# A transformer kernel on one core: sink-free attention scores get their mask from TensorE, banks are handed out in written order, and TensorE issues in written order

## The chip, the cores and the metric

One Trainium2 chip, one of its NeuronCores. The metric is the device time of one execution in microseconds (us). TensorE is called PE in the profile, with its weight loads listed apart as PEld; VectorE is DVE, ScalarE is ACT, GpSimd is POOL, SyncE (which issues most DMAs here) is SP.

## The reference

The kernel computes three things in a row. Attention works on 2 batches, 8 heads, 768 positions and 64 channels per head, with a window of 128 positions and 4 sink positions that every row may see:

```python
keep = is_sink | in_window          # in_window: 0 <= row - column < 128
scores = np.where(keep, scale * (q @ k.T), -1e9)
a = np.exp(scores - max(scores)); a = a / (sum(a) + 1e-9)
x = (a @ v) laid out as 1536 tokens x 512 channels
x = (silu(x @ w_gate) * (x @ w_val)) @ w_out            # d_ff 1536
g = x @ w_in; x = max(g, 0) + alpha * min(g, 0)         # d_ff 2048
out = x @ w_out2
```

## The kernel before

The attention is cut into 24 groups (class `Group`): one pair of heads by two blocks of 128 rows. A group that begins at row 0 of its batch (`i0 == 0`) needs no separate sink columns, because its keys already hold them; there are 8 of these sink-free groups. The 16 others carry a sink strip (`self.sink`). `ORDER` puts the groups in three passes of 8; a pass makes 512 tokens. The first pass holds just the 8 sink-free groups, first the four head pairs of batch 0, then the four of batch 1 (L814).

`attention` (L322) is a software pipeline over x = 0 to 26, written in this order for each x:

- `scores(x)`: PE multiplies q and k in fp32 into one PSUM bank for each head and block. DVE adds the mask and finds the row minimum of the negated scores in one instruction (L223), ACT takes the exponential of that bank and sums it (L227).
- `values(x-3)`: PE multiplies the transposed probabilities with v (L313, L316), ACT and DVE split the result into a high and a low half, `xh` (L805) and `xl` (L806).
- `flips(x-2)`: PE transposes probabilities (L272), and a sink strip (L295), into PSUM; ACT or DVE copies them out (L278, L280, L283), POOL cuts triangles (L284, L288).
- `norm(x)`: DVE adds and inverts the sums (L243, L244), POOL scales the probabilities (L250, L259).

Between these, `fast` weaves in the first feed-forward layer (`Moe1.unit`). From x = 10 on, after the first pass is done, `product()` issues one step of it: 12 matmuls of 128x512 in the fp32r format, of which one `pg` (gate), one `pv` (value) or one `po` (output) bank is made. There is one such step for each x before `values`, and one more after the flips of each x in `TWICE`. A gate bank needs all four head pairs of its pass: its 12 matmuls are three for each pair (`proj`, L609). A step also calls `st.tick()`, which converts one weight tile: ACT L520, DVE L536, L539 and L542, ACT L550, POOL or DVE L557. In the first pass only four weights are converted (`EARLY`).

DVE issues in written order (`manual_schedule`, L799). On PE, ACT and POOL a planner chooses the order ahead of time, and it chooses which of the 8 PSUM buffers a tile gets (one pool `ps`, L865). The chip then runs each engine's list in that order, with semaphores. After the attention the rest of the feed-forward work follows (`mix`), in which PE has nothing to wait for.

Of the kernel before, what the change touches and what calls it, by code (L numbers as in the profile page):

```python
# [16 lines left out]
P = 128  # L17
# [3 lines left out]
KD = DM // P  # L21
# [21 lines left out]
TWICE = (10, 12, 14, 16, 18, 20, 22, 25)  # L43
# [14 lines left out]

def setup(nc, tc, ctx, g):
# [7 lines left out]
    g.mask_0 = const.tile([P, P], F32, name="mask_0")  # L67
    g.mask_1 = const.tile([P, 2 * P], F32, name="mask_1")
    g.above = const.tile([P, P], I32, name="above")
    g.zero = const.tile([P, T], mybir.dt.bfloat16, name="zero")  # L70


def warm(nc, g, n):

    nc.vector.memset(g.zero, 0.0)
    ps = g.ps_m.tile([P, 512], F32, tag="ps", name="warm")
# [43 lines left out]
def first_masks(nc, g):  # L120
    win, snk = g.win, g.snk
    prev, cur = win[:, 0:P], win[:, P:]
    nc.vector.scalar_tensor_tensor(out=win, in0=g.rel, scalar=g.wd, in1=g.ge, op0=ALU.is_lt, op1=ALU.mult)
    nc.vector.tensor_scalar(out=snk, in0=g.key, scalar1=g.ns, scalar2=None, op0=ALU.is_lt)
    nc.vector.tensor_tensor(out=g.mask_0, in0=cur, in1=snk, op=ALU.max)
    bias(nc.vector, g.mask_0, g.mask_0)
    nc.vector.tensor_tensor(out=g.mask_1[:, 0:P], in0=prev, in1=snk, op=ALU.max)
    nc.vector.tensor_copy(g.mask_1[:, P:], cur)
    bias(nc.vector, g.mask_1, g.mask_1)
# [26 lines left out]
class Group:  # L156
    def __init__(self, nc, g, qk, vp, vs, b, hp, i0, put, cs, blk):
        self.nc, self.g = nc, g
        self.b, self.hp, self.i0, self.put = b, hp, i0, put
        self.cs, self.blk = cs, blk  # L160
        self.h0 = 2 * hp
        self.j0 = max(0, i0 - 1)
        self.nk = i0 + NG - self.j0
        self.sink = i0 + NG > 2
        self.off = 1 if i0 == 0 else 0
        self.qk_src, self.v_src = (x[min(i0, 1)] for x in (qk, vp))
        n = b * NPAIR + hp if i0 == 0 else (b * 2 + i0 // NG - 1) * NPAIR + hp
        self.qk_src, self.v_src = self.qk_src[n], self.v_src[n]
        self.vs_src = vs[b * NPAIR + hp]
        if self.sink:  # L170
# [29 lines left out]
    def scores(self, t):  # L200
        nc, g = self.nc, self.g
        i = self.i0 + t
        w, blk, sp, kk = self.blocks(t)
        lo, first = self.kpos[kk], P if sp is not None else 0
        if t == 0:
            self.ssum = g.st_p.tile([P, NG, 2], F32, tag="ssum", name="ssum")
            self.prb = g.pr_p.tile([P, 3 * 2 * P], F32, tag="pr", name="pr")
        p0 = self.prb_at(t)
        mask = g.mask_0 if i == 0 else g.mask_1 if i == 1 else g.mask_b if kk % 2 else g.mask_a
        pss = []  # L210
        for e in range(2):
            ps = g.ps_s.tile([P, 512], F32, tag="ps", name="ps_s")
            pss.append(ps)
        qs, ks = slice(self.qpos[t], self.qpos[t] + P), slice(lo, lo + first + w)
        for e in range(2):
            r = slice(e * D, (e + 1) * D)
            nc.tensor.matmul(pss[e][:, :first + w], self.th[r, qs], self.th[r, ks], start=True, stop=True)
        for e in range(2):
            ps = pss[e][:, first:first + w]
            if first:  # L220
                nc.vector.copy_predicated(ps[:, blk[0]:blk[0] + P], g.above, pss[e][:, 0:P])
            col = (self.b * H + self.h0 + e) * NQ + i
            nc.vector.tensor_tensor_reduce(  # L223
                out=ps, in0=ps, in1=mask, scale=-SCALE, scalar=3.0e38,
                op0=ALU.add, op1=ALU.min, accum_out=g.nb[:, col:col + 1],
            )
            nc.scalar.activation(  # L227
                self.prb[:, p0 + e * w:p0 + (e + 1) * w], ps, AF.Exp,
                bias=g.nb[:, col:col + 1], scale=-1.0, accum_out=self.ssum[:, t, e:e + 1]
            )  # L230
# [31 lines left out]
    def flip(self, t):  # L262
# [5 lines left out]
        ps = g.ps_t.tile([P, 512], F32, tag="ps", name="ps_p")  # L268
        for e in range(2):
            for x, c in enumerate(blk):  # L270
                y = (e * nb + x) * P
                nc.tensor.transpose(ps[:, y:y + P], self.pr(t, e, c, P), g.ident)  # L272
        b0 = max(0, 2 * t - self.off)
# [18 lines left out]
        if t == NG - 1 and self.sink:  # L292
            self.pts = g.pt_p.tile([P, P], F32, tag="pts", name="pts")
            ps = g.ps_t.tile([P, 512], F32, tag="ps", name="ps_p2")
            nc.tensor.transpose(ps[:, 0:P], self.sk.rearrange("p x s -> p (x s)"), g.ident)  # L295
            nc.scalar.activation(self.pts, ps[:, 0:P], AF.Copy)

    def values(self):
        nc, g, i0, n = self.nc, self.g, self.i0, NG
        xp = g.ps_x.tile([P, 512], F32, tag="ps", name="xp")  # L300
# [18 lines left out]
        self.put(xp[:, :n * P], self.hp, self.cs)  # L319


def attention(groups, begin):  # L322
# [12 lines left out]
    for x in range(n + LAG + 1):  # L335
        if x < n:
            for t in range(NG):
                groups[x].scores(t)
# [16 lines left out]
def verdict(nc, g):  # L355
# [9 lines left out]
    ps = g.ps_t.tile([P, 512], F32, tag="ps", name="ps_flag")  # L365
# [8 lines left out]
def dense(nc, tc, g, q, k, v, b):  # L374
    with ExitStack() as ctx:
# [17 lines left out]
        for hp in range(NPAIR):  # L393
# [4 lines left out]
            for e in range(2):  # L398
# [14 lines left out]
                for t in range(NQ):  # L413
                    ps = g.ps_t.tile([P, 512], F32R, tag="ps", name="dps_k")
# [6 lines left out]
            for i in range(NQ):  # L421
                ts = slice(i * P, (i + 1) * P)
                xp = g.ps_x.tile([P, 512], F32, tag="ps", name="dxp")
                for e in range(2):
                    src = sp.tile([P, S], F32, tag="src", name="dsrc")
                    for c0, n in ((0, 512), (512, 256)):
                        ps = g.ps_s.tile([P, 512], F32, tag="ps", name="dps_s")
# [17 lines left out]
                    for t in range(0, NQ, 2):  # L445
                        ps = g.ps_t.tile([P, 512], F32, tag="ps", name="dps_p")
# [161 lines left out]

def proj(nc, ps, w, xh, xl):  # L609
    wh, wl = w  # L610
    for kk in range(KD):
        c = slice(kk * P, (kk + 1) * P)
        nc.tensor.matmul(ps, wh[:, c], xh[:, kk], start=(kk == 0), stop=False)  # L613
        nc.tensor.matmul(ps, wh[:, c], xl[:, kk], start=False, stop=False)  # L614
        nc.tensor.matmul(ps, wl[:, c], xh[:, kk], start=False, stop=(kk == KD - 1))  # L615
# [14 lines left out]
class Moe1:  # L630
    def __init__(self, nc, g, st, base, xs, put):
        self.nc, self.g, self.st, self.base, self.xs, self.put = nc, g, st, base, xs, put
        self.accs = {}

    def unit(self, c, b):
# [10 lines left out]
        for x in range(0, CHUNK, 2):  # L646
            pair = hidden_pair(g)
            pss, sgs = [], []
            for r in range(2):
                ps = g.ps_m.tile([P, 512], F32, tag="ps", name="pg")  # L650
# [4 lines left out]
            for ps in pss:  # L655
                sg = g.t_p.tile([P, T], F32, tag="sg", name="sg")
                nc.scalar.activation(sg, ps, AF.Silu)
                sgs.append(sg)
            yield
            for r in range(2):  # L660
                hh, hl = (t[:, r] for t in pair)
                ps = g.ps_m.tile([P, 512], F32, tag="ps", name="pv")
                proj(nc, ps, st.get(at(1, x + r)), xh, xl)
                hid = g.t_p.tile([P, T], F32, tag="hid", name="hid")
                nc.vector.tensor_tensor(out=hid, in0=ps, in1=sgs[r], op=ALU.mult)  # L665
                split_hidden(nc, hid, hh, hl)
# [9 lines left out]
        for m in range(KD):  # L676
            mc = slice(m * P, (m + 1) * P)
            ps = g.ps_m.tile([P, 512], F32, tag="ps", name="po")
# [8 lines left out]
            else:  # L687
                nc.vector.tensor_tensor(out=av, in0=ps, in1=av, op=ALU.add)
            if c == nch - 1:
                split_hidden(nc, av, yh[:, m], yl[:, m])  # L690
# [8 lines left out]
class Moe2:  # L699
# [4 lines left out]
    def unit(self, c, b):  # L704
# [6 lines left out]
        for x in range(CHUNK):  # L711
# [4 lines left out]
            ph = g.ps_m.tile([P, 512], F32, tag="ps", name="ph")  # L716
# [15 lines left out]
        for t in range(T // P):  # L732
            ps = g.ps_m.tile([P, 512], F32, tag="ps", name="pf")
# [40 lines left out]

def fast(nc, tc, ctx, g, lim, alpha, qk, vp, vs, w_gate, w_val, w_out, x2_in, x2_out, out):
# [21 lines left out]
    with ExitStack() as inner:  # L797
        attention_pools(nc, tc, inner, g)
        inner.enter_context(tc.manual_schedule(engines={mybir.EngineType.DVE}))  # L799
# [14 lines left out]
        groups[:2 * NPAIR] = groups[0:2 * NPAIR:2] + groups[1:2 * NPAIR:2]  # L814
# [9 lines left out]
        for at, x, last in attention(groups, (begin_a, begin_b, begin_c)):  # L824
            done = max(0, last + (at != "before values"))
            if at == "values" and done in (per, 2 * per):
                ready.append(m1.unit(0, done // per - 1))
            if done < per:
                if at == "flips" and st.n_conv < EARLY:
                    st.tick(1 + (done > 1))  # L830
            elif at == "before values" or at == "flips" and x in TWICE:
                product()
    st.idle_pool = False
    for u in ready:
        for _ in u:
            st.tick()
# [6 lines left out]
def general(nc, tc, g, q, k, v, w_gate, w_val, w_out, x2_in, x2_out, out):  # L843
    g.exact = True
    with ExitStack() as ctx:
        xp = ctx.enter_context(tc.tile_pool(name="gx", bufs=1))
# [15 lines left out]
def build(nc, tc, q, k, v, w_gate, w_val, w_out, x2_in, x2_out, alpha, lim, qk0, qk1, v0, v1, vs, out):  # L862
    with ExitStack() as ctx:
        g = Ctx()
        ps = ctx.enter_context(tc.tile_pool(name="ps", bufs=8, space=PSUM))  # L865
        g.ps_m = g.ps_s = g.ps_t = g.ps_x = ps
# [71 lines left out]
```

## Time and profile before

| | us |
|---|---|
| median of 3 runs | 680.9 (680.4 to 681.8) |
| the profiled execution | 680.56 |
| its span, first to last instruction | 678.8 |
| PE busy in the span | 657.4 (97%) |
| DVE busy | 391.7 (58%) |
| ACT busy | 297.8 (44%) |
| POOL busy | 79.9 (12%) |

The span leaves out 1.76 us of the profiled execution's time. Busy times are of records; consecutive matmuls overlap in them, so how fast PE runs is read from the distance between the starts of matmuls. The mean granted PE clock over the span is 0.987 of full speed.

### The profile page before, as it was taken

Reading aid. Unit: us, or ns where it says so; the run is one execution under the profiler, and the core shown is the slowest. Engines: PE = TensorE matmul, PEld = TensorE weight load, DVE = VectorE, ACT = ScalarE, POOL = GpSimd, SP = SyncE. Lnnn points to the kernel's source line nnn. Section 1 sums busy time; section 2 is a strip of 40 time slices with the busy share of each in tenths; the row PEclk is TensorE's granted clock in tenths of the full one; section 3 lists DMA queues with packets and bytes.
Section 4 is the critical chain, followed back from the end, with each engine's and each line's share of the span. In section 5 each row is a group of like instructions: output and inputs, shape, how many; then the busy total and the mean of one; then the engine's idle time right before and its main releaser. Section 6 shows DMA issues by size and latency. Waiting matters only on the chain.

```text
span 678.8 us, 8589 instructions
## 1 busy us (share of the span) xinstructions
PE 657.4 (97%) x3098; PEld 519.5 (77%) x3098; DVE 391.7 (58%) x880; ACT 297.8 (44%) x680; POOL 79.9 (12%) x137
## 2 busy tenths in 40 slices
PE   7889889999999999999999999999999999999996
PEld 4555666767788888888888888888888888888885
DVE  5896858444289932389432789419834744334332
ACT  4778765656366612155221546336622333112320
POOL 3554644333100000000000000000000000000000
PEclk8989899999999999999999999999999999999998
DMA  9653535200045520045200034203400000000111
GB/s 264 180 169 115 166 114 168 69 24 24 1 155 186 169 79 1 0 125 181 68 0 1 33 124 129 89 1 93 156 1 0 1 0 1 1 0 8 55 63 67
DMA packets 37203, 52.29 MB, mean 77 GB/s; under 512 B 4384, under 2 KB 28960, under 8 KB 37152
## 3 DMA queue, kind: packets, MB, share of 16 engines
q1 hardware_dynamic: 34944, 51.65, 24.0%
q8 instruction: 26, 0.43, 0.2%
q10 hardware_dynamic: 2208, 0.01, 0.2%
q14 instruction: 25, 0.20, 0.1%
HBM read 48.51 MB, written 3.15 MB: 76 GB/s over the span
## 4 chain that ended last, share of the span: by engine, by line
PE 84%; DVE 7%; ACT 5%; issue 1%; POOL 1%; DMA 1%; SPq 0%; ACTq 0%; POOLq 0%
PE ph L615 6%; PE ph L613 6%; PE pf L739 6%; PE pf L737 6%; PE pf L738 6%; PE ph L614 6%; PE po L681 5%; PE po L682 5%; PE po L683 5%; PE pv L613 4%; PE pg L613 4%; PE pv L615 4%; PE pv L614 4%; PE pg L614 4%; PE pg L615 4%; PE xp L313 2%
## 5 line engine op out<-in xcount | busy, mean ns | idle before, releaser
L626 ACT ACTIVATE hh<-hid 128x512 fp32r<-128x512 f32 x84 | 53.1, 632 | 70.5 <-DVE hid L665 41.2
L627 DVE TENSOR_TENSOR hl<-hid,hh 128x512 fp32r<-128x512 f32 x84 | 57.9, 689 | 36.5 <-ACT hh L626 36.4
L613 PE MATMUL ph<-yh,wh 128*128 128x512 f32 x192 | 74.8, 390 | 0.0
L615 PE MATMUL ph<-yh,wl 128*128 128x512 f32 x192 | 74.7, 389 | 0.0
L737 PE MATMUL pf<-wh,hh 128*128 128x512 f32 x192 | 74.7, 389 | 0.0
L738 PE MATMUL pf<-wl,hh 128*128 128x512 f32 x192 | 74.7, 389 | 0.0
L614 PE MATMUL ph<-yl,wh 128*128 128x512 f32 x192 | 74.7, 389 | 0.0
L719 ACT ACTIVATE neg<-ph,sal 128x512 f32<-128x512 f32 x48 | 33.0, 687 | 93.4 <-PE ph L615 93.4
L739 PE MATMUL pf<-wh,hl 128*128 128x512 f32 x192 | 72.1, 389 | 0.0
L550 ACT ACTIVATE wh<-w_m 128x512 fp32r<-128x512 f32 x68 | 42.6, 630 | 55.8 <-DVE w_m L542 17.4
L721 DVE SCALAR_TENSOR_TENSOR hid<-ph,sig,neg 128x512 f32<-128x512 f32 x48 | 35.9, 749 | 38.4 <-ACT neg L719 38.0
L613 PE MATMUL pg<-xh,wh 128*128 128x512 f32 x144 | 57.6, 401 | 0.0
L613 PE MATMUL pv<-xh,wh 128*128 128x512 f32 x144 | 56.9, 395 | 0.3 <-ACT pt L283 0.3
L614 PE MATMUL pg<-xl,wh 128*128 128x512 f32 x144 | 57.0, 396 | 0.0
L615 PE MATMUL pg<-xh,wl 128*128 128x512 f32 x144 | 56.6, 393 | 0.0
L681 PE MATMUL po<-hh,wh 128*128 128x512 f32 x144 | 56.5, 394 | 0.0
L614 PE MATMUL pv<-xl,wh 128*128 128x512 f32 x144 | 56.2, 391 | 0.0
L682 PE MATMUL po<-hh,wl 128*128 128x512 f32 x144 | 56.2, 391 | 0.0
L615 PE MATMUL pv<-xh,wl 128*128 128x512 f32 x144 | 56.1, 390 | 0.0
L744 DVE TENSOR_TENSOR acc<-pf,acc 128x512 f32<-128x512 f32 x36 | 23.2, 686 | 52.0 <-PE pf L739 52.0
L683 PE MATMUL po<-hl,wh 128*128 128x512 f32 x144 | 53.2, 390 | 0.0
L557 DVE TENSOR_TENSOR wl<-w_m,wh 128x512 fp32r<-128x512 f32 x56 | 38.2, 686 | 21.6 <-ACT wh L550 21.5
(106 smaller groups left out, 1198.0 us busy)
## 6 DMA issues: line engine op xcount, KB each, us to landing
w_raw<-in_moe_w_out SPq DMA_DIRECT2D x28, 512.0 KB, 3.4
w_raw<-in_moe_w_in SPq DMA_DIRECT2D x16, 512.0 KB, 3.8
w_raw<-in_moe_w_gate SPq DMA_DIRECT2D x12, 512.0 KB, 3.7
w_raw<-in_moe_w_val SPq DMA_DIRECT2D x12, 512.0 KB, 3.6
th<-in_qk SPq DMA_DIRECT2D x16, 336.0 KB, 3.0
vr<-in_v SPq DMA_DIRECT2D x16, 192.0 KB, 2.4
out<-acc SPq DMA_DIRECT2D x12, 256.0 KB, 2.2
th<-in_qk SPq DMA_DIRECT2D x8, 256.0 KB, 5.5
```

The costliest lines, as they stand in the source:

```text
L550: nc.scalar.activation(wh, m, AF.Copy)
L613: nc.tensor.matmul(ps, wh[:, c], xh[:, kk], start=(kk == 0), stop=False)
L614: nc.tensor.matmul(ps, wh[:, c], xl[:, kk], start=False, stop=False)
L615: nc.tensor.matmul(ps, wl[:, c], xh[:, kk], start=False, stop=(kk == KD - 1))
L626: nc.scalar.activation(hh, hid, AF.Copy)
L627: nc.vector.tensor_tensor(out=hl, in0=hid, in1=hh, op=ALU.subtract)
L681: nc.tensor.matmul(ps, wh[:, mc], hh, start=(x == 0), stop=False)
L682: nc.tensor.matmul(ps, wl[:, mc], hh, start=False, stop=False)
L683: nc.tensor.matmul(ps, wh[:, mc], hl, start=False, stop=(x == CHUNK - 1))
L737: nc.tensor.matmul(ps, hh[:, ts], wh, start=(x == 0), stop=False)
L738: nc.tensor.matmul(ps, hh[:, ts], wl, start=False, stop=False)
L739: nc.tensor.matmul(ps, hl[:, ts], wh, start=False, stop=(x == CHUNK - 1))
```

## The change

PSUM becomes one tile of 8 banks that the kernel hands out itself in the order in which the program is written (`Banks`: the bank given back longest ago is taken first). In the first pass scores have banks 0 to 3, taken by twos, transposes and values have banks 4 to 6, and bank 7 is for the first gate. PE joins DVE in `manual_schedule`, so PE issues in written order too. When the attention is over, the tile is released and an ordinary pool of 8 buffers takes its place; a pool that lands on the bytes of a released one lets all its buffers wait for every user of the old one.

A sink-free group puts both blocks of a head side by side in one bank (128 and 256 columns). PE first writes the mask into it, as the product of an identity and `mask_f`, and adds the scores to it. DVE then takes two row maxima over both heads at once and scales them once; ACT's exponential reads the bank with the scale.

The first pass goes by head pair: batch 0 and batch 1 of pair 0, then of pair 1, and so on. When both groups of a pair are split, `m1.part` issues the three matmuls of that pair for the first gate bank, so that the gate's 12 matmuls stand at x = 4, 6, 8 and 10, and the step at x = 10 has none left. `TWICE` has one entry less. The steps left over after x = 26 are issued inside the region where PE is in written order. The transposed sink strip goes into the bank of the group's second transposes in place of a bank of its own.

```diff
-TWICE = (10, 12, 14, 16, 18, 20, 22, 25)
+TWICE = (10, 13, 16, 18, 20, 22, 25)
...
+class Banks:
+    def __init__(self, pool):
+        self.all = pool.tile([P, 8, 512], F32, name="banks")
+        self.free = list(range(8))
+        self.held = {}
+
+    def take(self, n=1, among=range(8)):
+        for i in self.free:
+            if i % n == 0 and i in among and all(j in self.free for j in range(i, i + n)):
+                break
...
+        for j in range(i, i + n):
+            self.free.remove(j)
...
+    def give(self, ap):
+        self.free += self.held.pop(id(ap))[1]
...
 def identities(nc, g):
     make_identity(nc, g.ident)
+    nc.gpsimd.tensor_copy(g.identr, g.ident)
...
+    bias(nc.vector, g.mask_f[:, 0:P], both)
...
+    bias(nc.vector, g.mask_f[:, P:2 * P], g.rel[:, P:])
+    bias(nc.vector, g.mask_f[:, 2 * P:], cur)
...
+    def free_scores(self):
         nc, g = self.nc, self.g
+        ps = g.banks.take(2, range(4))
+        for e in range(2):
+            nc.tensor.matmul(ps[:, e, :3 * P], g.identr, g.mask_f, start=True, stop=False, skip_group_check=True)
+        cols = [slice(0, P), slice(P, 3 * P)]
+        for t, c in enumerate(cols):
+            for e in range(2):
+                r = slice(e * D, (e + 1) * D)
+                nc.tensor.matmul(
+                    ps[:, e, c], self.th[r, self.qpos[t]:self.qpos[t] + P], self.th[r, 0:(t + 1) * P],
+                    start=False, stop=(t == 1), skip_group_check=True,
+                )
+        top = ps[:, :, 510:512]
+        for t, c in enumerate(cols):
+            nc.vector.tensor_reduce(out=top[:, :, t], in_=ps[:, :, c], axis=AX.X, op=ALU.max)
+        nc.vector.tensor_scalar(out=self.nb, in0=top, scalar1=-SCALE, scalar2=None, op0=ALU.mult)
+        for t, c in enumerate(cols):
+            for e in range(2):
+                self.exp(ps[:, e, c], t, e, SCALE)
+        give(g, ps)
...
-            ps = g.ps_t.tile([P, 512], F32, tag="ps", name="ps_p2")
-            nc.tensor.transpose(ps[:, 0:P], self.sk.rearrange("p x s -> p (x s)"), g.ident)
-            nc.scalar.activation(self.pts, ps[:, 0:P], AF.Copy)
+            nc.scalar.activation(self.pts, ps[:, 2 * P:3 * P], AF.Copy)
...
+    def part(self, kk):
+        if kk == 0:
+            self.begun = bank(self.g, "pg", (7,))
+        proj_part(self.nc, self.begun, self.st.get(self.base), *self.xs[0], kk)
...
-        inner.enter_context(tc.manual_schedule(engines={mybir.EngineType.DVE}))
+        g.banks = Banks(inner.enter_context(tc.tile_pool(name="bank", bufs=1, space=PSUM)))
+        inner.enter_context(tc.manual_schedule(engines={mybir.EngineType.DVE, mybir.EngineType.PE}))
...
-        groups[:2 * NPAIR] = groups[0:2 * NPAIR:2] + groups[1:2 * NPAIR:2]
...
+            if at == "flips" and 0 < done <= per and done % 2 == 0:
+                m1.part(done // 2 - 1)
...
+        while ready:
+            product()
     st.idle_pool = False
-    for u in ready:
-        for _ in u:
-            st.tick()
+    psum_pool(tc, ctx, g)
```

## Rows read from the trace of the kernel before

**Rows 1.** Windows by stage: length; busy us (instructions) PE PEld DVE ACT POOL; PEclk, DMA, GB/s

```profile
0.00:48.50 48.50, 39.66 (x213) 23.92 (x214) 38.36 (x158) 30.55 (x116) 23.50 (x37) 0.89 0.69 204
48.50:182.60 134.10, 127.58 (x725) 90.14 (x724) 74.46 (x260) 82.98 (x235) 56.41 (x100) 0.99 0.29 90
```

**Rows 2.** The same view: a PE gap, the stretch after it, and a dense one

```profile
77.00:79.00 2.00, 0.33 (x1) 0.14 (x1) 1.93 (x5) 1.97 (x5) 0.70 (x1) 1.00 0.51 154
79.00:84.50 5.50, 5.44 (x16) 3.88 (x17) 4.02 (x17) 5.21 (x19) 4.09 (x7) 0.70 0.43 143
...
300.00:400.00 100.00, 100.00 (x443) 82.81 (x442) 58.87 (x101) 35.60 (x62) 0.00 (x0) 1.00 0.21 70
```

**Rows 3.** Waits of PE, 48.5 to 182.6 us: waiting <- waited for: us, times, longest

```profile
PE ps_s L217 <- ACT pr L227: 2.5, 2, 1.5
PE ps_p L295 <- ACT pr L227: 1.7, 1, 1.7
```

**Rows 4.** Timeline of all engines at the start: start, us, instruction, idle before

```profile
5.20 1.34 PE L217 MATMUL ps_s<-th 64*128 64x128 f32 x8
...
6.95 0.52 DVE L105 TENSOR_SCALAR mask<-mask 128x256 f32<-128x256 f32 x1
...
7.38 0.28 DVE L223 CUSTOM_DVE_ANT_0 ps_s<-ps_s,mask 128x128 f32<-128x128 f32 x1
...
7.76 0.37 ACT L227 ACTIVATE pr<-ps_s,nb 128x128 f32<-128x128 f32 x1 [4.75 <-DVE nb L223]
...
10.40 0.17 DVE L243 TENSOR_SCALAR rinv<-ssum 128x4 f32<-128x4 f32 x1 [1.67 <-ACT pr L227]
...
12.82 0.17 DVE L243 TENSOR_SCALAR rinv<-ssum 128x4 f32<-128x4 f32 x1 [0.78 <-ACT pr L227]
```

**Rows 5.** Timeline of DVE, x = 4 (to 25.13) and x = 8

```profile
22.41 0.42 DVE L806 TENSOR_TENSOR xl<-xp,xh 128x256 fp32r<-128x256 f32 x1 [0.84 <-ACT xh L805]
22.75 0.68 DVE L278 COPY pt<-ps_p 128x512 f32<-128x512 f32 x1
23.35 0.42 DVE L536 TENSOR_SCALAR w_m<-w_m 128x512 int32<-128x512 int32 x1
...
25.13 0.17 DVE L243 TENSOR_SCALAR rinv<-ssum 128x4 f32<-128x4 f32 x1
...
41.77 0.42 DVE L806 TENSOR_TENSOR xl<-xp,xh 128x256 fp32r<-128x256 f32 x1
...
43.00 0.28 DVE L221 COPY_PREDICATED ps_s<-above,ps_s 128x128 f32<-128x128 int32 x1
```

**Rows 6.** Waits of DVE up to 48.5 us

```profile
DVE xl L806 <- ACT xh L805: 2.1, 2, 1.3
```

**Rows 7.** Timeline of PE: scores of x = 9, then three stretches of the mixed stage

```profile
38.43 1.16 PE L217 MATMUL ps_s<-th 64*128 64x288 f32 x4
...
120.35 0.87 PE L313 MATMUL xp<-pt,vr 128*64 128x256 f32 x8
...
122.92 0.48 PE L614 MATMUL pg<-xl,wh 128*128 128x512 f32 x1
...
129.72 1.09 PE L313 MATMUL xp<-pt,vr 128*64 128x256 f32 x12
...
131.92 1.24 PE L217 MATMUL ps_s<-th 64*128 64x288 f32 x8
...
136.04 0.87 PE L313 MATMUL xp<-pt,vr 128*64 128x256 f32 x8
```

**Rows 8.** Timeline of all engines: a last output bank of the attention's region

```profile
180.86 0.39 PE L683 MATMUL po<-hl,wh 128*128 128x512 f32 x1
...
181.28 0.60 ACT L686 ACTIVATE acc<-po 128x512 f32<-128x512 f32 x1 [2.12 <-PE po L683]
```

**Rows 9.** Groups by line up to 200 us: changes to Silu's table

```profile
L657 ACT ACT_TABLE_LOAD x8 | 10.3, 1283 | 0.1
```

**Rows 10.** Timeline of POOL: the last cut before the values at 136.04

```profile
134.66 0.41 POOL L288 TENSOR_SCALAR_AFFINE_SELECT pt<-pt 128x256 f32<-128x256 f32 x1
```

More of the change, by code (lines that the diff above doesn't have):

```diff
@@ L56, with bank, give @@
     pass
+class Banks:
[7 more added lines that the diff above has]
+                break
+        else:
+            assert False, self.free
+        for j in range(i, i + n):
+            self.free.remove(j)
+        ap = self.all[:, i:i + n] if n > 1 else self.all[:, i]
+        self.held[id(ap)] = (ap, range(i, i + n))
+        return ap
+    def give(self, ap):
+        self.free += self.held.pop(id(ap))[1]
+def bank(g, name, among=range(8)):
+    return g.banks.take(1, among) if g.banks else g.ps.tile([P, 512], F32, tag="ps", name=name)
+def give(g, ap):
+    if g.banks:
+        g.banks.give(ap)
 def setup(nc, tc, ctx, g):
@@ L169, in __init__ @@
         self.vs_src = vs[b * NPAIR + hp]
+        self.banks = range(8) if self.sink else range(4, 7)
         if self.sink:
@@ L198, in blocks, with begin @@
         return KW, [0], P, kk
-    def scores(self, t):
-        nc, g = self.nc, self.g
-        i = self.i0 + t
-        w, blk, sp, kk = self.blocks(t)
[L204 to L214, printed above, removed]
+    def begin(self):
+        g = self.g
+        self.ssum = g.st_p.tile([P, NG, 2], F32, tag="ssum", name="ssum")
+        self.prb = g.pr_p.tile([P, 3 * 2 * P], F32, tag="pr", name="pr")
+        self.nb = g.nb.rearrange("p (h i) -> p h i", i=NQ)[:, self.b * H + self.h0:][:, :2, self.i0:self.i0 + NG]
@@ new lines, in exp, with scores @@
+    def exp(self, src, t, e, scale):
+        o = self.prb_at(t) + e * src.shape[1]
+        self.nc.scalar.activation(
+            self.prb[:, o:o + src.shape[1]], src, AF.Exp, bias=self.nb[:, e, t:t + 1], scale=scale,
+            accum_out=self.ssum[:, t, e:e + 1],
+        )
+    def scores(self):
+        self.begin()
+        if self.sink:
+            for t in range(NG):
+                self.sink_scores(t)
+        else:
+            self.free_scores()
+    def free_scores(self):
+        nc, g = self.nc, self.g
+        ps = g.banks.take(2, range(4))
[8 more added lines that the diff above has]
+                    start=False, stop=(t == 1), skip_group_check=True,
+                )
+        top = ps[:, :, 510:512]
[5 more added lines that the diff above has]
+                self.exp(ps[:, e, c], t, e, SCALE)
+        give(g, ps)
@@ L215, in scores, with sink_scores @@
+    def sink_scores(self, t):
+        nc, g = self.nc, self.g
+        w, blk, sp, kk = self.blocks(t)
+        lo = self.kpos[kk]
+        pss = [bank(g, "ps_s") for e in range(2)]
+        qs, ks = slice(self.qpos[t], self.qpos[t] + P), slice(lo, lo + P + w)
         for e in range(2):
             r = slice(e * D, (e + 1) * D)
-            nc.tensor.matmul(pss[e][:, :first + w], self.th[r, qs], self.th[r, ks], start=True, stop=True)
+            nc.tensor.matmul(pss[e][:, :P + w], self.th[r, qs], self.th[r, ks], start=True, stop=True)
@@ L227, in scores @@
[L227 to L230, printed above, removed]
+                out=ps, in0=ps, in1=g.mask_b if kk % 2 else g.mask_a, scale=-SCALE, scalar=3.0e38,
+                op0=ALU.add, op1=ALU.min, accum_out=self.nb[:, e, t:t + 1],
+            )
+            self.exp(ps, t, e, -1.0)
+            give(g, pss[e])
     def prb_at(self, t):
@@ L267, in flip @@
         nb = len(blk)
-        ps = g.ps_t.tile([P, 512], F32, tag="ps", name="ps_p")
+        ps = bank(g, "ps_p", self.banks)
         for e in range(2):
@@ L336, in attention @@
         if x < n:
-            for t in range(NG):
-                groups[x].scores(t)
+            groups[x].scores()
         yield "before values", x, x - LAG - 1
@@ L649, in unit @@
             for r in range(2):
-                ps = g.ps_m.tile([P, 512], F32, tag="ps", name="pg")
+                if self.begun is not None and (c, b, x, r) == (0, 0, 0, 0):
+                    pss.append(self.begun)
+                    continue
+                ps = bank(g, "pg")
                 proj(nc, ps, st.get(at(0, x + r)), xh, xl)
```

72 lines of the change are left out of this document (40 added, 32 removed).

## The prediction

> **What bounds the kernel now.** I read the windows by stage first. After the attention PE runs dense, 443 matmuls in 100 us, so 0.226 us for each [rows 2], and nothing in the change touches that stage. What can move lies in two stages. In the *first pass* (to 48.5 us) PE has no feed-forward work; it has records for 39.7 of 48.5 us, and DVE, in written order, is the busiest in effect with 38.4 us, while each of its steps also waits for ACT [rows 1]. This stage is a chain, not a load. In the *mixed stage* (48.5 to 182.6 us) PE is the bound: it idles 134.1 - 127.6 = 6.5 us [rows 1], mostly for a PSUM buffer that an exponential or a Silu still reads (2.5 us of scores, 1.7 us of a transposed sink strip, and smaller ones [rows 3]), and one of these gaps is followed by 5.5 us at a mean clock of 0.70 [rows 2]. With levels of 1.2 and 2.4 GHz that is 3.3 us at the lower one, a loss of 1.65 us. So 8.2 us of the mixed stage are not work. The sum below is made against the profiled execution, 680.56 us (span 678.8 and 1.76 around it), which is 0.3 us under the median of the runs.
>
> **First gate early: -2.0 us.** Three matmuls each for three head pairs, 9 in all, leave the place where PE becomes the bound: 9 x 0.226 = 2.03 us. The last three stay at x = 10, where PE would wait for the last pair anyway. Bounds: nothing, if the hole that they leave stays open, and 2.7 us for all twelve.
>
> **What the early gate waits for: +2.0 us.** This is a new wait, and it is at the head of PE's list. `m1.part` at x = 4, 6, 8 needs `xl(x-3)`, which DVE makes only after its own `scores(x)`. Behind it stands `scores(x+1)`. Before, PE was an iteration ahead: the scores of x = 9 began at 38.43, 3.3 us before DVE made the `xl` of x = 8 at 41.77 [rows 5, 7]. Now they come after it: three matmuls (0.68) and scores (half of a sink group's from 38.43 took 1.16 at a lower clock [rows 7], a whole one from 131.92 took 1.24), 2.0 us with the handover. At x = 4 and x = 6 DVE is covered meanwhile: from the end of `xl` at about 22.8 the probability copy and a weight conversion last to 25.13, and two small instructions to about 25.4 [rows 5], 2.6 us; if PE is at its lower clock the 1.9 us of work become 3.8, so 0 to 1.3 us show each time. At x = 8 there is no conversion: DVE wants the next scores at 43.00, 0.9 us after the `xl` [rows 5], so 1.0 to 2.9 us show. I take 0.3, 0.3 and 1.4; bounds 1.0 and 5.5. The cover of the first two is the weight conversion; without it each would cost what x = 8 does.
>
> By the Trainium skill, *PSUM — Partial Sum Buffer*, section "Engine vs sequencer instructions", matmuls start and complete in program order, so what stands behind a waiting matmul can't pass it. By that rule the 2.0 us stand; if PE could let the scores pass they would be 0. The row of x = 9 shows only that the planner had put nothing in front of those scores.
>
> **Sink-free scores, the start: +1.5 us.** Before, the scores of group 0 were done at 6.54 while DVE was still making the mask, which ended at 7.47, and DVE began at 7.38 on the part that was ready [rows 4]. Now PE needs the mask first: it ends at about 7.25 (the copy and the wide bias at 6.95 give way to two narrow ones), then come two mask matmuls and the scores. A 384-column mask matmul is in no row; bounds are 0.226 (a 512-column one) and nothing, and by columns it is 0.17. With 0.34 for two and 1.34 for the scores (5.20 [rows 4]) DVE begins at 8.9, 1.5 us later. Bounds: 1.0, if PE is faster than at 5.20, and 2.4, if it is at its lower clock throughout. Later mask matmuls, 14 x 0.17 = 2.4 us, cost nothing as long as PE idles there (8.8 us [rows 1]); without that cover 2.4.
>
> **Sink-free scores, the chain: +1.3 us.** Before, the first exponential began 0.38 us after DVE's first instruction (7.38 to 7.76), and the chain scores, exponentials, sums, next scores took 12.82 - 10.40 = 2.42 us [rows 4]. Now all four exponentials wait for both maxima and the scaling. A row maximum out of PSUM is in no row. By the nearest, reads of 256 and 512 columns take 0.42 and 0.68 us, and the next begins after 0.34 and 0.60 [rows 5]; with 0.2 for the scaling 1.14, with the handover 1.24. So the chain is 0.86 us longer: 3.3. That shows in full at x = 1, where DVE has nothing else. At x = 3, 5 and 7 DVE's `xl` and copy (0.94 us [rows 5]) or a conversion lie in the gap: 0.2 us each taken there, at most 0.9; at x = 2, 4, 6 a conversion of 1.8 us hides it. DVE's own work stays about the same. Sum 1.3, bounds 0.9 and 3.5.
>
> **ACT order in the first pass: -1.0 us.** DVE waited 2.1 us in two iterations because ACT ran exponentials before the split [rows 6]. While DVE now takes maxima ACT is free for it. Half taken, bounds -2.1 and 0.
>
> **Written order and banks, the mixed stage: -4.0 us of 8.2.** Each iteration takes eight to nine banks and the oldest is reused, so scores(x+1) need exponentials of x, one iteration older than the buffers on which PE stood. Between the two PE has values and transposes, 2.2 us from 129.72 to 131.92 [rows 7], and one step or two of 12 x 0.226 = 2.7 us: 4.9 or 7.6 us. DVE's eight instructions of about 0.3 us (the one at 43.00 took 0.28 [rows 5]) and a last exponential of 0.4 make 2.8; a change to Silu's table and back adds 2 x 1.28 [rows 9]: 5.4 us, more than an iteration with one step, less than one with two. `TWICE` puts two of the four pairs of Silus (x = 20, 22) in double iterations and two (x = 11, 14) in single ones. So half of the loss goes. Bounds: all 8.2 gone, or none and new waits (rival 3).
>
> **Fewer splits: -1.0 us.** Where the planner ran transposes inside the values, the stretch from 120.35 to 122.92 holds one `pg` matmul more than that from 129.72 to 131.92 [rows 7]: 2.57 - 0.23 - 2.20 = 0.14 us worse. There are seven such places in the timeline.
>
> **The end of the region: +1.1 us.** The new pool's buffers wait for the last reader of the old tile. That is ACT's copy of the last `po` bank: 181.28 began 0.42 us after the last matmul's start and lasted 0.60 [rows 8]; with 0.1 to hand over and less the 0.226 that a matmul lasts anyway, PE stands still 0.9 us, 1.1 with a copy queued behind the last split of attention.
>
> The clock could add to this. After the gap at 77 to 79 us (0.33 us of PE in 2.0) it fell to a mean of 0.70, which cost 1.65 us [rows 2]. The Trainium skill, *TensorE: Matmul & The Clock Gate*, section "Why this matters for your kernels", advises against idle gaps between bursts of matmuls for that reason; if the rule bites here, the term is 2.75 and the sum 1.65 higher. The row agrees that a gap can do it, and its gap is the longer one, so I keep 1.1.
>
> **Free edits.** The sink strip in a shared bank leaves PE's work as it is. Loads on SP keep size, number and lead when the groups change place. The fp32r identity is one POOL instruction while POOL waits for the limits.
>
> **Sum.** -2.0 + 2.0 + 1.5 + 1.3 - 1.0 - 4.0 - 1.0 + 1.1 = -2.1, so 680.56 - 2.1 = 678.5 us.
>
> **Rivals.**
> 1. *The waits vanish.* Written order gives each bank its longest rest, all 8.2 us go, and ACT's order gains 2.1: 680.56 - 2.1 - 4.2 - 1.1 = 673.2; with the part waits at 1.0, 672. For it: no wait in rows 3 is on work that PE lacks. Against: table changes stay.
> 2. *A wash.* Part waits at the lower clock (4.5 in place of 2.0): 681.0. For it: the mean clock of the first pass is 0.89 [rows 1]. Against: PE has more work there now.
> 3. *Slower: PE stands before the values.* In written order all of values(x-3) come before flips(x-2), with no filler. In the trace the scores at 131.92 lead the values at 136.04 and the last triangle cut ended at 135.07 [rows 7, 10]: a slack of 0.97 us. A table change there and back (2.56) ahead of the copies overruns it by 1.6, and there were eight changes [rows 9]. If the old waits stay and two of the eight overrun: 678.5 + 4.0 + 3.2 = 685.7. It decides early: without the saving of 4.0 the other terms are +1.9, so if waits and clock still lose 8.0 of the 8.2 us, the time is 682.3 and the kernel slower by 0.2%.
>
> **Chances and range.** Forecast (675 to 679.5) 0.38; rival 1 0.17; rival 2 (679.5 to 682.3) 0.20; rival 3 0.25. A difference of 0.2%, 1.36 us, is about what a measurement of this kernel can tell from none. So faster 0.55, same 0.20, slower 0.25. The range reaches from rival 1's 672 less 1 to rival 3's 685.7: 671 to 685.5. For the forecast alone it is 675 to 680.
>
> **What would show it.** In the changed profile: the first `rinv` at 11.4 to 12.8 in place of 10.40, its next 3.3 us later; `scores(9)` right after a `pg` triple; DVE waiting for PE there; PE's waits from the first dense gate to the last `po` near 3 us and one low-clock stretch at most; a PE gap of 0.9 to 1.2 us before the first `pg` after the region. I am wrong if the waits of values on POOL's cuts appear in PE's list (rival 3), or if PE's triples never hold up DVE.

## The result: slower by 1.1%

| | before | after |
|---|---|---|
| median of 5 runs, us | 680.9 (680.4 to 681.86) | 688.49 (687.76 to 690.04) |
| ratio, 95% interval | | 1.0107 [1.0084, 1.013] |
| span of the profiled execution, us | 678.8 | 688.1 |

The forecast was 678.5 us, the range 671 to 685.5. The changed kernel's profiled execution, 690.04 us, is the slowest of its five. In one experiment below (TensorE left to the planner in the changed kernel) five of ten runs were in a slower state of the chip, and its figures are of the other five.

Where do the 9.3 us of span come from? First the windows by stage, which answer to [rows 1, 2]: length, busy time of PE, PEld, DVE, ACT and POOL with counts, then granted clock, DMA share and GB/s.

```profile
0.00:48.50 48.50, 36.99 (x224) 21.18 (x224) 33.97 (x104) 29.33 (x111) 22.39 (x36) 0.96 0.67 201
48.50:99.70 51.20, 46.49 (x256) 32.62 (x255) 37.23 (x123) 35.92 (x105) 28.15 (x39) 0.97 0.44 133
99.70:115.00 15.30, 8.43 (x33) 4.78 (x33) 11.08 (x28) 6.26 (x19) 6.94 (x8) 0.67 0.43 127
115.00:192.00 77.00, 75.02 (x445) 55.61 (x442) 30.07 (x121) 43.21 (x121) 25.84 (x56) 0.98 0.15 45
300.00:400.00 100.00, 100.00 (x443) 82.81 (x442) 59.69 (x102) 37.18 (x68) 0.00 (x0) 1.00 0.21 65
```

The dense stage is what it was. The hole is one stretch, 99.7 to 115 us: PE is busy for 8.4 of 15.3 us, at a mean clock of 0.67, while DVE works 11.1. The timeline of PE shows what stands there (start, duration, instruction, idle before and what ended it):

```profile
99.79 0.50 PE L766 MATMUL banks<-hh,wh 128*128 128x512 f32 x1
...
103.71 0.56 PE L766 MATMUL banks<-hh,wh 128*128 128x512 f32 x1 [2.27 <-ACT wh L619]
106.44 0.80 PE L767 MATMUL banks<-hh,wl 128*128 128x512 f32 x1 [2.16 <-POOL wl L626]
...
109.11 0.80 PE L766 MATMUL banks<-hh,wh 128*128 128x512 f32 x1 [1.44 <-ACT wh L619]
110.89 0.80 PE L767 MATMUL banks<-hh,wl 128*128 128x512 f32 x1 [0.99 <-POOL wl L626]
...
112.05 1.98 PE L382 MATMUL banks<-pt,vr 128*64 128x256 f32 x12
...
115.09 0.48 PE L766 MATMUL banks<-hh,wh 128*128 128x512 f32 x1
...
125.51 0.50 PE L766 MATMUL banks<-hh,wh 128*128 128x512 f32 x1
...
130.49 0.47 PE L681 MATMUL banks<-xh,wh 128*128 128x512 f32 x1
```

This is the first output bank, at x = 16. Two of its four weights are not converted, so PE waits for each one's high half (ACT L619) and low half (POOL L626): 2.27 + 2.16 + 1.44 + 0.99 = 6.9 us. The values at 112.05 stand behind them in written order, though the last cut of the probabilities that they read (POOL L358) ended at 102.46. From one product to the next these 12 matmuls, values and transposes take 15.30 us; the same work takes 4.98 further on (125.51 to 130.49). So 10.3 us are lost here, waits and low clock together.

In the kernel before, the same bank starts at 100.91, so up to here the changed kernel was 1.1 us ahead, and the next bank starts at 106.51:

```profile
100.91 0.50 PE L681 MATMUL po<-hh,wh 128*128 128x512 f32 x1
...
102.87 0.40 PE L683 MATMUL po<-hl,wh 128*128 128x512 f32 x1
103.19 1.09 PE L313 MATMUL xp<-pt,vr 128*64 128x256 f32 x12
...
105.93 0.50 PE L681 MATMUL po<-hh,wh 128*128 128x512 f32 x1
```

There the planner had put values and transposes between the ninth matmul (102.87) and the tenth (105.93), the first that needs the last weight.

The weights' conversions on DVE (first instruction of each):

```profile
91.21 0.66 DVE L605 TENSOR_SCALAR w_m<-w_m 128x512 int32<-128x512 int32 x1
...
100.76 0.63 DVE L605 TENSOR_SCALAR w_m<-w_m 128x512 int32<-128x512 int32 x1
...
105.94 0.72 DVE L605 TENSOR_SCALAR w_m<-w_m 128x512 int32<-128x512 int32 x1
...
107.36 0.43 DVE L605 TENSOR_SCALAR w_m<-w_m 128x512 int32<-128x512 int32 x1
```

Those at 100.76 and 105.94 are the 11th and 12th, the ones that PE waits for; the 12th stands behind scores(16). Before, the 12th began at 101.19. Two things make it late. **A lost step:** `part` begins the first gate bank early, and `unit` then passes over it

```python
                if self.begun is not None and (c, b, x, r) == (0, 0, 0, 0):
                    pss.append(self.begun)
                    continue
```

together with the `yield` that stands at its end. The first step at x = 10 is thus the second gate bank (not a step with nothing left, as the section on the change has it), and one `st.tick()`, one conversion, is gone from the count ahead of the output bank. **Work pulled in:** the conversion at 107.36 is the 13th. There is room for 12 in the attention; it belongs to the steps behind it, which no written order holds, and the planner put it (and a 14th at 111.67) between DVE's instructions here. The same stood in the kernel before, at 102.86 and 109.50.

### The profile page after: what moved, and what is told of

The parts are those of the page before. It is cut to its first block, busy times and chain, and to the rows that moved or that the text cites. A ratio compares the mean times of both kernels' runs of the same rounds, so it can differ in the third digit from the quotient of the medians.

```text
span 688.1 us, 8596 instructions
## 1 busy us (share of the span) xinstructions
PE 657.0 (95%) x3114; PEld 519.5 (76%) x3114; DVE 391.4 (57%) x840; ACT 298.5 (43%) x680; POOL 83.3 (12%) x138
## 4 chain that ended last, share of the span: by engine, by line
PE 83%; DVE 9%; ACT 4%; issue 2%; POOL 1%; DMA 1%; ACTq 0%; DVEq 0%
PE ph L683 6%; PE pf L825 6%; PE ph L682 6%; PE pf L824 6%; PE pf L823 6%; PE ph L681 6%; PE pg L681 4%; PE pv L681 4%; PE pg L683 4%; PE pv L683 4%; PE po L768 4%; PE po L766 4%; PE po L767 4%; PE pg L682 4%; PE pv L682 4%; ACT pr L245 2%
## 5 line engine op out<-in xcount | busy, mean ns | idle before, releaser
L619 ACT ACTIVATE wh<-w_m 128x512 fp32r<-128x512 f32 x68 | 42.5, 630 | 62.3 <-DVE w_m L611 24.0
L626 DVE TENSOR_TENSOR wl<-w_m,wh 128x512 fp32r<-128x512 f32 x56 | 38.1, 686 | 21.4 <-ACT wh L619 21.1
L611 DVE SCALAR_TENSOR_TENSOR w_m<-w_raw,w_m 128x512 uint32<-128x512 uint32 x68 | 47.1, 694 | 0.9
L245 ACT ACTIVATE pr<-banks,nb 128x160 f32<-128x160 f32 (+2 forms) x96 | 37.9, 401 | 21.6 <-DVE nb L292 10.3
L681 PE MATMUL pg<-xh,wh 128*128 128x512 f32 x112 | 43.7, 390 | 0.9 <-DVE xl L898 0.9
L589 ACT ACTIVATE w_m<-w_raw 128x512 f32<-128x512 f32 x52 | 34.9, 671 | 22.2 <-DVE wl L626 10.8
L682 PE MATMUL pg<-xl,wh 128*128 128x512 f32 x112 | 43.6, 389 | 0.0
L683 PE MATMUL pg<-xh,wl 128*128 128x512 f32 x112 | 43.6, 389 | 0.0
L681 PE MATMUL pv<-xh,wh 128*128 128x512 f32 x112 | 43.6, 389 | 0.0
L682 PE MATMUL pv<-xl,wh 128*128 128x512 f32 x112 | 43.6, 389 | 0.0
L683 PE MATMUL pv<-xh,wl 128*128 128x512 f32 x112 | 43.6, 389 | 0.0
```

What stands on the lines that cost most here:

```text
L245: self.nc.scalar.activation(self.prb[:, o:o + src.shape[1]], src, AF.Exp, bias=self.nb[:, e, t:t + 1], scale=scale, accum_out=self.ssum[:, ...
L611: nc.vector.scalar_tensor_tensor(out=mu, in0=lo.bitcast(U32), scalar=29, in1=mu, op0=ALU.logical_shift_right, op1=ALU.bitwise_or)
L619: nc.scalar.activation(wh, m, AF.Copy)
L626: eng.tensor_tensor(out=wl, in0=m, in1=wh, op=ALU.subtract)
```

## The experiments

All ratios are to the kernel before, run on the same chip as the experiment; the changed kernel's own is 1.0107. Experiments are compared by their ratios.

**One and two conversion steps more.** Edit, the second `tick` in the second run only:

```diff
                 m1.part(done // 2 - 1)
+                if done == per:
+                    st.tick()
...
             elif at == "before values" or at == "flips" and x in TWICE:
+                if at == "before values" and x == 14:
+                    st.tick()
                 product()
```

> The changed kernel with one more weight conversion step, issued at x = 10 behind the last gate part; nothing else. Theory 1 (a lost step: the gate bank that was begun early skips a yield, so one st.tick() fewer stands before the first output bank, and its last weight is converted one iteration late): the conversion of the last out weight moves from behind scores(16) to x = 15, where it starts at about 101 us, and PE waits for one weight in place of two, about 4.4 of the 6.9 us and part of the low clock: 682 to 685 us. Theory 2 (PE's written order alone: nothing may pass a waiting output matmul, and the conversions are on time for any other order): no change from one step, 687 to 689. Theory 3 (the conversions are late because VectorE is overloaded between 95 and 110 us): an extra conversion earlier takes time from VectorE and gains under 1 us.

> The same with a second extra conversion step, at x = 14 ahead of the feed-forward step. Theory 1: the last out weight is converted a whole iteration before its use, the four waits of the first output bank (2.27 + 2.16 + 1.44 + 0.99 us) and the low clock behind them go. That stretch took 15.3 us from the first output matmul to the next bank, where the same work takes 4.98 further on, so 10.3 us at most come back: 678 to 680 us. Theory 2: 686 or more. Theory 3: within 1 us of the run with one step.

Measured: 687.03 us, 1.0075 [1.0058, 1.0092], and 686.03, 1.0064 [1.0047, 1.0081]. A gain in the direction of theory 1, but 2 to 3 us in place of 4 to 10, and only the interval of two steps is clear of the changed kernel's. With two steps no output matmul waits for a weight any more, yet the stretch stays slow. Waits of PE from 48.5 to 192 us in that run (total, times, longest), and its DVE timeline:

```profile
PE banks L288 <- ACT pr L245: 4.0, 4, 1.4
PE banks L382 <- POOL pt L358: 3.0, 2, 2.3
```

```profile
94.87 0.62 DVE L605 TENSOR_SCALAR w_m<-w_m 128x512 int32<-128x512 int32 x1
...
96.56 0.16 DVE L310 TENSOR_SCALAR rinv<-ssum 128x4 f32<-128x4 f32 x1
...
101.33 0.41 DVE L605 TENSOR_SCALAR w_m<-w_m 128x512 int32<-128x512 int32 x1
```

The pulled-in conversions now begin at 94.87 and 101.33, among the sums of x = 14 (96.56) and the scores of x = 15. DVE is busy for 17.5 of the 20 us from 90 to 110, and the chain scores, exponentials, cuts, values is late instead.

**VectorE relieved.** On the run with two steps: no weight from the 13th on is started in the attention, their first ACT instruction reads its scale from a tile that DVE writes at its end, and the slopes move.

```diff
-        if not self.begun and self.n_load > self.n_start:
+        if not self.begun and self.n_load > self.n_start and not (self.idle_pool and self.n_start >= WB):
             self.start()
...
+        if WB <= i < WB + 3 and not g.exact:
+            scale = g.late
...
-        if x == 14:
+        if x == 20:
             begin[2]()
...
+        nc.vector.memset(g.late, DOWN)
         assert not g.banks.held
```

> The run with two extra conversion steps, and VectorE relieved between 90 and 106 us: the conversions of weights 12 to 14, which the planner had pulled from behind the attention into that stretch (two of about 2 us), stay behind it, and the slopes and range tests move from x = 14 to x = 20. Theory 3: from the sums of x = 14 to those of x = 16 it takes 13 us in place of 16.9, the low clock behind 96 us goes, and the kernel is 3 to 5 us faster than with two steps alone, within 0.3% of before. Theory 2: the attention chain (exponentials, scaling, cuts) is what PE waits for, and under 1.5 us come back.

Measured: 680.41 us, 0.9982 [0.9965, 0.9999], 5.6 us below two steps alone. From 90 to 110 us PE now works at full clock. The windows, with two steps alone and relieved:

```profile
90.00:110.00 20.00, 15.60 (x57) 10.58 (x56) 17.48 (x52) 9.17 (x32) 10.86 (x14) 0.75 0.51 166
```

```profile
90.00:110.00 20.00, 18.29 (x104) 13.50 (x105) 14.13 (x51) 11.13 (x40) 13.24 (x20) 1.00 0.47 146
```

> The run with two extra steps and only the conversions of weights 12 to 14 kept behind the attention; slopes and range tests stay at x = 14. The two parts of the lean run gave 5.6 us together. The two conversions hold VectorE for 2 x 2 us, the slopes and tests for about 1.2 us of work: I expect 3.5 to 4.5 us of the 5.6 from the conversions, 681.5 to 682.5. If the slopes carry it (they stand ahead of scores(15) and wait), it is 684 or more.

Measured: 681.75 us, 1.0006 [0.9995, 1.0017]: 4.0 of the 5.6 us come from the pulled-in conversions (0.0058 of 681), the rest from the slopes and tests.

**Relief without the steps, and relief of the kernel before.** The same edit on the changed kernel, and on the one before.

> The changed kernel with VectorE relieved, without the two extra conversion steps. Theory 1 (lost step): PE still waits for the last out weight at the first output bank, 3 to 4 us slower than the lean run with steps: 683 to 685. If the conversion was late only because VectorE was full, this run equals the lean run with steps, 680 to 681, or is faster, since the first pass is spared a conversion.

> The kernel before with VectorE relieved between 90 and 110 us as in the lean run (conversions of weights 12 to 14 kept behind the attention, slopes and range tests at x = 20), nothing of the change. If the pull-in of conversions costs any order of PE the same, it is 4 to 6 us faster than before (675 to 677). If it is the written order of PE that makes the VectorE stretch expensive, because the planner's order had other work for PE there, it gains 0 to 2 us (679 to 681).

Measured: 688.92 us, 1.0102 [1.0074, 1.0131], and 683.33, 1.0029 [1.0014, 1.0044]. Alone the relief gives nothing: without the steps PE waits as ever (view as above),

```profile
PE banks L769 <- ACT wh L622: 3.6, 2, 2.4
PE banks L770 <- POOL wl L629: 2.8, 2, 2.2
```

and the kernel before does not profit: it is 0.3% slower, which its expectation did not allow for. Steps alone gave 0.0043, relief alone 0.0005, both 0.0125: the two are in series, and removing one uncovers the other.

**Who issues in what order.** TensorE left to the planner in the changed kernel; and put into written order in the kernel before (one line each, `engines={...}`).

> The changed kernel with TensorE left to the planner again (only VectorE in written order); the conversion step is still missing. Theory 1 taken alone: the weight comes as late as before, so most of the wait stays, 685 or more, though other work can stand in it. Theory 2: the planner puts values, transposes and scores into the wait, the low clock does not come, and 6 to 10 us come back: 678 to 682. If both are needed for the loss, this run and the one with two steps both come out near 679 to 681.

> The kernel before with one edit: PE in written order beside VectorE. Buffers, scores, gate, pair order, TWICE and conversion steps are those of before. Theory 2 (PE's written order is what costs in the mixed stage, because a PE that waits can't take other work): 5 to 9 us slower than before. Theory 1 (only the lost conversion step): within 2 us of before. Theory 3 (VectorE is full between 85 and 106 us and sets the pace in any order): also slower, but only around x = 14 to 16, by 3 to 6 us between the sums of those iterations.

Measured: 689.56 us (five runs from 683.79 to 692.71), 1.0097 [1.0062, 1.0132], and 684.57, 1.0043 [1.0028, 1.0058].

In the first, free order did not bring the time back. Still, theory 2 is not out: in the trace no output matmul waits for a weight, and the granted clock is 1.00 from 48.5 to 192 us. The stall is gone, but the planner puts the scores by twos among feed-forward matmuls, and PE reaches the first output bank at 107.56, 7.8 us later than the changed kernel. The same 128 score records keep PE busy for 32.2 us in place of 25.1; groups by line and shape, 30 to 195 us, planned and then changed kernel:

```profile
L288 PE MATMUL banks<-th 64*128 64x288 f32 x128 | 32.2, 447 | 2.9 <-ACT pr L245 2.8
```

```profile
L288 PE MATMUL banks<-th 64*128 64x288 f32 x128 | 25.1, 438 | 4.0 <-ACT pr L245 3.9
```

In the second the weight wait appears although no step is lost; at 2.9 us slower it lies between theories 1 and 2 (waits of PE, 48.5 to 192 us):

```profile
PE po L681 <- ACT wh L550: 2.8, 1, 2.8
PE po L682 <- POOL wl L557: 2.0, 1, 2.0
```

So the conversions of before were just in time too; the planner had filled the wait.

**The prediction's terms, in the kernel as changed:** gate whole (no `part`, `TWICE` of before); old sink-free scores; parts one iteration later. The edit of the last:

```diff
-            if at == "flips" and 0 < done <= per and done % 2 == 0:
+            if (at == "before values" and 0 < done < per and done % 2 == 0) or (at == "flips" and done == per):
                 m1.part(done // 2 - 1)
```

> The changed kernel without the early gate: all 12 matmuls of the first gate bank stand at x = 10 as a step of their own, with the conversion step that belongs to it, and TWICE is that of the kernel before. Banks, packed scores, pair order and PE's written order stay. Theory 1: the missing step is back, the time falls by 4 to 9 us, to 679 to 685, though 9 matmuls (2.0 us) return to the dense part. Theory 2: 688 to 690. As to the wait that the prediction set against the early gate (2.0 us): if it is that large, this run is no slower than the one with one step; if it is small, it is 2 us slower.

> The changed kernel with the sink-free scores of before (mask added by VectorE, two banks for each block out of banks 0 to 3); all else as changed, the conversion step still missing. By the prediction's terms (1.5 for the start, 1.3 for the longer chain) the first sums come at 10.4 to 10.9 us in place of 12.85, their next 2.4 later, and the kernel is 2 to 3 us faster than the changed one: 685.5 to 686.5. If the first pass has slack behind x = 2 (conversions, the wait for the gate parts), it is under 1 us.

> The changed kernel with the first three gate parts issued one iteration later, behind scores(x+1) in place of ahead of them; the fourth stays at x = 10. By the prediction (2.0 us for what the gate parts hold up) VectorE no longer waits for the scores of x = 9 and the sums of x = 10 come 1 to 2 us earlier than 55.41; the kernel is 1 to 2 us faster than the changed one. If the parts never held up VectorE, the sums of x = 5 to 10 stay where they are and so does the time.

Measured: 689.77 us, 1.0117 [1.0101, 1.0134]; 687.6, 1.009 [1.0061, 1.012]; 688.81, 1.0103 [1.0068, 1.0138]. None is told apart from the changed kernel. With the gate whole the missing step is back, yet nothing came of it: theory 1 alone fails again. In its trace PE waits 1.9 us for weights in place of 6.9, but 5.4 us in place of 2.9 before scores, for exponentials.

**The terms once the conversions are on time.** First the relieved run with old scores, as base; then the base with TensorE planned, with the banks kept to the end, with the gate whole; and the kernel before with written order, relief and one step.

> The lean run with the two extra steps, and the sink-free scores of before. By the run with old scores alone (1.2 us) it is 1 to 2 us faster than the lean run: 678.5 to 679.5. If the packed scores' cost is taken up by the gate parts and the table changes later, the same as the lean run.

> The run with old scores, two extra steps and a relieved VectorE, with TensorE left to the planner. If PE's written order pays once the conversions are on time (the prediction's terms: waits -4.0, splits -1.0), this is 3 to 8 us slower than 678.6 and its scores stand split among feed-forward matmuls. If written order is still the burden, it is faster, 675 to 678.

> The same run as base, with the tile of banks kept to the end of the fast path in place of a new pool behind the attention; the feed-forward layers take and give banks by hand there too. PE's wait of 0.93 us ahead of the first gate bank behind the attention (for the last reader of the old tile) goes: 0.5 to 1.2 us faster than 678.6, if the fixed banks cost nothing in the dense stage.

> The base run without the early gate: 12 gate matmuls at x = 10 as a step with its own conversion, the extra one at x = 14 kept, TWICE of before. The prediction had the early gate at -2.0 for nine matmuls moved and +2.0 for what they hold up: within 0.7 us of 678.6. If the parts' waits are covered by conversions (the run with parts later showed no gain), it is 1 to 2 us slower.

> The kernel before (pool of buffers, old scores, gate whole, old pair order) with PE in written order, a relieved VectorE and one extra conversion step at x = 14. If lateness of the conversions is all that written order cost there (4.8 us of waits in the run of before with written order), the 2.9 us that this run was slower come back and more: 678 to 680, level with the base run. If the banks in written order are needed as well, 681 to 684.

| run | median us | ratio, 95% interval |
|---|---|---|
| base | 678.63 | 0.9954 [0.9938, 0.997] |
| TensorE planned | 698.17 | 1.0242 [1.0206, 1.0279] |
| banks kept | 677.58 | 0.9939 [0.9912, 0.9966] |
| gate whole | 682.0 | 1.0002 [0.9986, 1.0018] |
| before, written, relieved | 679.96 | 0.9966 [0.995, 0.9983] |

Base, banks kept and the kernel before with written order and relief have intervals below 1; the first two are not told apart. TensorE planned is 0.0288, 19.6 us, slower than base, where 3 to 8 us were expected. That prices the planner's order with banks that are handed out in written order, not order by itself. Scores stand alone there among feed-forward matmuls; the timeline of that run, then of the changed kernel:

```profile
78.85 0.75 PE L284 MATMUL banks<-th 64*128 64x288 f32 x2
79.53 0.50 PE L679 MATMUL banks<-xh,wh 128*128 128x512 f32 x1
```

```profile
118.02 1.24 PE L288 MATMUL banks<-th 64*128 64x288 f32 x8
119.19 0.50 PE L766 MATMUL banks<-hh,wh 128*128 128x512 f32 x1
```

Two records alone take 0.68 us from start to next start, eight together 1.17, so 0.29 for two. The 128 score records keep PE busy for 32.4 us, in base for 24.8: 7.6 of the 11.8 us between the two profiled executions (690.43 and 678.63). The other four planned runs took 696.8 to 699.9 us, and no trace shows why. With the banks kept, the feed-forward matmuls follow the last strip values without a gap:

```profile
181.89 0.71 PE L381 MATMUL banks<-pts,vsr 128*128 128x128 f32 x4
182.36 0.47 PE L681 MATMUL banks<-xl,wh 128*128 128x512 f32 x1
```

## Why the prediction was wrong

The step that failed is **"Written order and banks, the mixed stage: -4.0 us of 8.2"**. It asked of each bank whether its last reader was done, and never of each matmul whether its operands were there. The weights of the first output bank were just in time already, and what had covered them was the planner's freedom, which the change takes away. Rival 3 had the mechanism (PE in written order stands where there is no filler) and the wrong place: ahead of values, where the changed kernel shows 0.8 us for POOL's cuts, while the weights take 6.9. Its place turns up once the weights are on time: 3.0 us with two steps alone. That its price, 685.7, came within 2.8 us is luck, for it was added up from other waits. The conversion step that the early gate took along, 0.0032 or 2.2 us by the run with one step, was in no count of what "First gate early" moves. PE's waits of this stage were to be near 3 us with one low-clock stretch at most. Apart from the weights they came to 3.7 us, with a clock of 0.52 from 158.5 to 161.9, some 1.6 us more: 5.3 of the 8.2 us are left where about 4.2 were forecast. By the Trainium skill, *PSUM — Partial Sum Buffer*, section "Engine vs sequencer instructions", matmuls start and complete in program order; the trace agrees, with the values at 112.05 behind the last late weight, and the prediction applied that rule to the gate parts alone.

Was the term itself wrong? With the conversions on time, written order takes the kernel before from 1.0029 to 0.9966, some 4.3 us, against the -5.0 of waits and splits together. From the kernel before itself it is 0.0034, 2.3 us. That run has one conversion step more as well, so the share of order alone is not separated. The waits for exponentials did shrink little: 2.9 us in scores, against 2.5 and 1.7 of a strip [rows 3].

**First gate early, -2.0, and its wait, +2.0.** That PE "would wait for the last pair anyway" at x = 10 was misread. In the kernel before, the nine matmuls stood in that place from 48.57 on while the last pair was being split (its `xl` ran from 49.45 to 49.87). In the changed kernel the hole that they leave stays open, which was one of the term's own bounds; the two timelines, before first:

```profile
48.57 0.48 PE L613 MATMUL pg<-xh,wh 128*128 128x512 f32 x1
```

```profile
52.90 0.80 PE L681 MATMUL banks<-xh,wh 128*128 128x512 f32 x1 [1.37 <-ACT xh L897]
```

PE waits 1.37 us, and from 52.9 to 56.1 the clock is 0.50, 1.6 us more. In base the waits at this place are 0.7 us. With the conversions on time the early gate gives 0.0048, 3.3 us net (gate whole against base; that pair differs in one `TWICE` entry too). PE stands at the parts as foreseen, and scores(9) come right after them, but VectorE loses little:

```profile
43.93 0.50 PE L682 MATMUL banks<-xl,wh 128*128 128x512 f32 x1 [1.61 <-DVE xl L898]
...
44.59 1.24 PE L288 MATMUL banks<-th 64*128 64x288 f32 x8
```

DVE began on these scores at 45.38 after 0.62 us of waiting, where 1.4 was taken, and the run with parts later gained nothing that shows. The 2.0 was too large.

**Start +1.5, chain +1.3.** All engines at the start of the changed kernel, against [rows 4]:

```profile
7.63 0.59 PE L262 MATMUL banks<-mask_f,identr 128*128 128x384 f32 x2 [2.41 <-DVE mask_f L140]
...
8.15 1.43 PE L267 MATMUL banks<-th 64*128 64x128 f32 x8
...
9.64 1.17 DVE L273 TENSOR_REDUCE banks<-banks 128x2 f32<-128x256 f32 x2 [2.16 <-PE banks L267]
...
12.85 0.17 DVE L310 TENSOR_SCALAR rinv<-ssum 128x4 f32<-128x4 f32 x1 [1.85 <-ACT pr L245]
...
16.32 0.17 DVE L310 TENSOR_SCALAR rinv<-ssum 128x4 f32<-128x4 f32 x1 [1.84 <-ACT pr L245]
```

The first `rinv` at 12.85 is at the edge of 11.4 to 12.8, the next 3.47 later (3.3 forecast). The chain's own parts, 0.86 and three times 0.2, make 1.5 rather than 1.3. Two mask matmuls took 0.52 us, not 0.34, and DVE began at 9.64, not 8.9. The mechanism held. The price at the end seems smaller than 2.8: 0.0017 in the changed kernel and 0.0028 (1.9 us) in the relieved one, but in both the intervals of the runs compared overlap.

**ACT order -1.0.** The wait of DVE for `xh` fell from 2.1 us [rows 6] (2.4 up to 60 us) to 1.2 up to 60 us: right. **The end of the region +1.1.** The first `pg` behind the attention:

```profile
192.06 0.50 PE L681 MATMUL pg<-xh,wh 128*128 128x512 f32 x1 [0.93 <-DVE xl L898]
```

It waits 0.93 us, for the last split rather than ACT's copy, and the clock stays at 1.00. Keeping the banks removes that wait; the 0.0015 that it gives is within the intervals.

Open stays why, with the gate whole and conversions on time, the changed kernel (1.0002) is behind the one before with written order (0.9966). Banks, pair order, the strip's bank and the region's end differ between them, and only the last, 0.93 us of some 2.5, was seen.

## What to carry to other kernels

Before an engine goes into written order, list for every instruction the last of its operands to be made, not only the buffer that it writes: what a planner had covered with other work becomes a stall there, with all the chains behind it. When a step of a paced loop disappears, count what else was tied to it, here a weight conversion. Of two delays in series, removing one shows little or nothing; remove both before a theory is dropped.

## What was not expected of the hardware

A pair of score records alone among 128x512 matmuls takes 0.68 us, in a group of eight 0.29: such a split costs 0.39 us, where the prediction took 0.14 for one inside the values. Over the 128 records this came to 7.1 and 7.6 us in the two traces with TensorE planned.

The granted clock fell to a mean of 0.67 over the stretch with waits of 1 to 2.3 us one after another (99.7 to 115 us), but it doesn't take several. This single gap, with scores on either side of it, came after a stretch without a wait since 115 us, and the clock was 0.52 from 158.5 to 161.9:

```profile
157.46 0.75 PE L288 MATMUL banks<-th 64*128 64x288 f32 x2 [1.11 <-ACT pr L245]
```

In the kernel before, a gap of 1.05 us ahead of 149.96 in the same place between scores left it at 1.00, and so did the one of 0.93 us at 192.06 in the changed kernel. Which of such gaps brings the clock down was not foreseen, and these runs do not tell.
